# Nystrom attention with a mixing MLP: PSUM columns in runs, the pseudo-inverse in 32x32 blocks, another decode of the weights

## The chip, the cores and the metric

The kernel runs on one core of one Trainium2 chip. The metric is the device time of one execution in microseconds. Before the change three runs took 1086.55, 1086.78 and 1087.39 us, so the median is 1086.78 us. One further execution was profiled; the durations below come from it.

## The reference

The reference has two parts. The first is attention through 32 landmarks per head (8 batches, 8 heads, 576 tokens, 64 columns per head):

```python
A = sm(q, k_lm); Bm = sm(q_lm, k_lm); C = sm(q_lm, k)      # 576x32, 32x32, 32x576
Z = Bm.transpose(0, 1, 3, 2) / (norm_1(Bm) * norm_inf(Bm) + 1e-06)
for _ in range(6):
    Z = 2 * Z - Z @ Bm @ Z                                  # pseudo-inverse of Bm
attn = A @ Z @ C @ v
```

The second takes the heads side by side as `x` (8 x 576 x 512), adds the real part of its two-dimensional Fourier transform, normalises each row and puts it through a two-layer MLP (512 to 2048 to 512) with a residual:

```python
u = x + real(fft(fft(x, axis=1), axis=2))
out = u + relu(layernorm(u) @ w_ch1) @ w_ch2
```

The weights arrive as 64-bit floats.

## The kernel before

**Numbers.** Large products are made of three 16-bit matmuls each: a value is kept as a high half and a low half (`split`, line 208: ScalarE writes the high half with a scale, VectorE subtracts it and writes the low half), and `mm3` (line 203) multiplies high by high, high by low and low by high. The landmark part is 32-bit.

**Three strands.** Generators run side by side under a planner with a clock of its own (`run`, line 845): `attention` (priority 1), which calls `tokens` for a batch and spawns its `landmarks`; `weights` (priority 2); `mlp` (priority 3), which fills what is left of TensorE. Only TensorE's order is written out by the planner; the other engines' instructions stand in about the order in which the strands issue them, and each engine works its own queue in order. The planner's costs are those of `Timed` and `mm`; `till` says how long a strand waits before it comes back for a result.

**Weights** (`weights`, line 232). The 2 x 16 pieces of the two matrices (128 x 512 each) are decoded from 64-bit to 32-bit floats. For each piece ScalarE takes the magnitude of the high words into a `row` buffer, GpSimd raises it to a floor (`MIN64`), and VectorE does three integer operations: a shift by 3 and mask, an or with the top two bits, an or with the low word shifted by 29. After the next piece ScalarE sums the magnitudes of each row of the decoded piece (`bound`), which gives the power of two by which a matrix is scaled. When all of the first matrix is decoded, `scale(0)` makes that factor, and from then on one piece of the first matrix is halved (`halve`: one `split`) with each piece of the second that is decoded. After the last piece comes `scale(1)`, and then the 16 pieces of the second matrix are halved one after the other. The halves of piece f overwrite the place where the source of piece f - 1 lay, so that a high half cannot be written before the halving ahead of it is done.

**Attention, tokens** (`tokens`, line 346). Softmax rows, transposes, and the Fourier transform along the tokens: for each of two parts x and two groups g, `mm3` writes 160 columns into a PSUM tile twice, even columns and odd columns (`pss[g][:, o:320:2]`), with tables `t1`; then the 32 left-over tokens are added over all 320 columns (`t1t`), and the result is split into `CS`. That is 24 matmuls of 160 columns in a batch, 12 for each part.

**Attention, landmarks** (`landmarks`, line 477). `B` (32 x 32 per head, four heads below each other in the 128 partitions, two groups) and `C` are made; then B is laid out block-diagonally as `Bbd` (128 x 128), transposed by TensorE to `BT`, `E = I - c B B^T` is made as 128 x 128 block-diagonal matrices, and six rounds multiply E with `RE` (E's 32 columns of each head and the 64 columns of the right-hand side C v); VectorE spreads the new E over the block diagonal again each time. The last product is with `Bbd`. Everything behind it in the batch (the matrices `Wx`, `Wt`, `WC`, then `mix`, `norm`) waits for that.

**MLP** (`mlp`, line 777). 18 steps of 256 tokens, each with 8 times 24 matmuls of 256 columns (`h`) and 8 times 12 of 512 columns (`acc`). The first product needs the first matrix in halves and normalised rows of batch 0, the second needs the second matrix in halves.

## Time and profile before

| | |
|---|---|
| median of three runs | 1086.78 us |
| the profiled execution | 1085.87 us |
| its span, first to last instruction | 1084.1 us |
| TensorE busy | 995.0 us of the span |
| VectorE busy | 621.2 us |
| ScalarE busy | 350.8 us |
| GpSimd busy | 166.4 us |
| mean granted TensorE clock | 0.959 |

The profiled execution lies 0.9 us below the median, and 1.8 us of its time lie outside the span. In the profile PE is TensorE, PEld its weight loads, DVE VectorE, ACT ScalarE, POOL GpSimd. A row of a group names line, engine, operation, output and inputs by the program's tile names, shapes, count, then busy time in us and the mean in ns of one. Nearly all instructions carry the lines of helpers (196 matmul, 201 transpose, 121 the timed engines), so that groups are told apart by their tiles: `t<-`/`at<-t,mid` are the 160-column products, `at<-RE,E` a round of the inverse, `w<-w,wsc` a halving, `row<-row` of 128x512 the shift (DVE) or the floor (POOL) of the decode, `row<-w,row` and `w<-w,row` the two or-operations. A 32-bit matmul is recorded as two instructions. Times in a timeline are from the span's start, and the start of the next row says when an engine was free for it.

### The profile page before, as it was taken

The page shows a single profiled execution, that of the slowest core. Times are in us where ns is not written, and L with a number is a line of the kernel's source. Part 1 is how long each engine was busy: PE and PEld are TensorE (multiplying, and loading weights), DVE is VectorE, ACT ScalarE, POOL GpSimd, SP SyncE. Part 2 cuts the span into 40 slices and gives each one's busy share as a digit, 9 for nine tenths or more (in the row PEclk, how much of TensorE's full clock was granted, in tenths as well). Part 3 has the DMA queues.
Part 4 walks back from the last instruction along what each step waited for, and adds up shares of the span by engine and source line. Part 5 has one row for each costly group of instructions (what it writes and reads, how often), then busy time and mean ns, then how long its engine had stood idle before and what let it go on. Part 6 is the DMA issues. An engine that isn't in the chain of part 4 may idle for free.

```text
span 1084.1 us, 19661 instructions
## 1 busy us (share of the span) xinstructions
PE 995.0 (92%) x8062; PEld 695.2 (64%) x8062; DVE 621.2 (57%) x1673; ACT 350.8 (32%) x797; POOL 166.4 (15%) x157
## 2 busy tenths in 40 slices
PE   3245688999999999999999999999999999999998
PEld 2233554677776677766776677767676676766665
DVE  7988989768553466446646574566552563441111
ACT  4557656324231333123232332143312332111110
POOL 2764502021111020110202020112010020110000
PEclk9565799999999999999999999999999999999999
DMA  9734502222101130010402030113110000110000
GB/s 334 235 110 148 148 25 89 69 45 103 60 26 30 47 116 21 20 35 16 156 2 49 11 127 31 40 21 121 48 40 20 21 1 21 21 41 13 17 20 20
DMA packets 71018, 68.16 MB, mean 63 GB/s; under 512 B 41360, under 2 KB 59792, under 8 KB 70800
## 3 DMA queue, kind: packets, MB, share of 16 engines
q1 hardware_dynamic: 70928, 66.91, 20.0%
q8 instruction: 63, 1.03, 0.4%
q14 instruction: 27, 0.22, 0.1%
HBM read 48.02 MB, written 9.44 MB: 53 GB/s over the span
## 4 chain that ended last, share of the span: by engine, by line
PE 84%; DVE 11%; ACT 2%; issue 1%; DMA 1%; POOL 1%; SPq 0%; ACTq 0%; POOLq 0%
PE h L196 33%; PE acc L196 33%; PE at L196 16%; DVE w L121 3%; DVE row L121 2%; PE at L201 2%; DVE mid L121 1%; DMA w<-w_dram 1%; ACT mid L121 1%; ACT row L121 1%; DVE u L121 1%; DVE big L121 0%; ACT w L121 0%; DVE lm L121 0%; DVE asum L121 0%
## 5 line engine op out<-in xcount | busy, mean ns | idle before, releaser
L196 PE MATMUL h<-unT,w 128*128 128x256 f16 x3456 | 413.9, 274 | 17.5 <-DMA unT<-row 13.4
L196 PE MATMUL acc<-w,h 128*128 128x512 f16 x1680 | 395.1, 379 | 0.0
L196 PEld LDWEIGHTS <-w 128*128 128x128 f16 x3456 | 337.5, 99 | 88.5 <-DMA unT<-row 14.2
L196 PEld LDWEIGHTS <-h 128*128 128x128 f16 x1680 | 161.8, 98 | 160.9 <-issue 4.1
L121 DVE SCALAR_TENSOR_TENSOR h<-h 128x512 f16<-128x512 f32 x140 | 96.3, 688 | 246.7 <-ACT h L121 246.3
L121 ACT ACTIVATE h<-h 128x512 f16<-128x512 f32 x140 | 83.4, 596 | 359.0 <-PE h L196 358.6
L121 POOL TENSOR_TENSOR r<-ve,mhalf 128x2 f32<-128x2 f32 (+1 forms) x20 | 13.8, 690 | 417.5 <-DVE ve L121 417.4
L121 POOL TENSOR_SCALAR row<-row 128x512 f32<-128x512 f32 x32 | 54.9, 1729 | 57.1 <-ACT row L121 45.9
L196 PEld LDWEIGHTS <-mid 128*128 128x128 f16 x432 | 50.8, 119 | 18.4 <-issue 7.9
L121 POOL TENSOR_TENSOR mid<-mid,asum 128x512 f32<-128x512 f32 x14 | 14.8, 1055 | 276.9 <-DVE asum L121 276.9
L196 PEld LDWEIGHTS <-big 128*128 128x128 f16 (+1 forms) x768 | 40.1, 102 | 25.9 <-DVE big L121 10.8
L121 POOL TENSOR_TENSOR row<-row 128x512 f16<-128x512 f32 (+1 forms) x44 | 45.1, 1038 | 36.1 <-ACT row L121 36.1
L121 ACT CAST row<-row 128x512 f16<-128x512 f32 (+1 forms) x44 | 23.3, 558 | 71.6 <-DVE row L121 69.9
L121 DVE SCALAR_TENSOR_TENSOR row<-at,scw,row 128x262 f32<-128x262 f32 (+1 forms) x48 | 21.3, 486 | 43.7 <-ACT row L121 29.9
L121 DVE TENSOR_REDUCE lm<-big 128x32 f32<-128x576 f32 (+1 forms) x48 | 44.0, 943 | 3.9 <-DMA big<-k_dram 3.5
L121 ACT ACTIVATE row<-w 128x512 f32<-128x512 f32 x54 | 34.4, 642 | 33.1 <-DVE w L121 21.1
L196 PE MATMUL at<-RE,E 128*128 128x96 f32 (+1 forms) x192 | 30.8, 285 | 12.1 <-DVE RE L121 12.1
L196 PEld LDWEIGHTS at<-RE,E 128*128 128x128 f32 x192 | 28.4, 202 | 17.8 <-DVE RE L121 13.9
L121 DVE SCALAR_TENSOR_TENSOR u<-at,scw,row 128x128 f32<-128x128 f32 (+3 forms) x120 | 38.9, 388 | 0.0
L196 PE MATMUL at<-mid,big 128*128 128x262 f16 (+1 forms) x288 | 34.4, 288 | 4.6 <-DVE mid L121 2.3
L121 POOL TENSOR_TENSOR mid<-mid 128x256 f32<-128x256 f32 (+1 forms) x32 | 33.0, 1035 | 21.0 <-ACT mid L121 12.2
L121 DVE SCALAR_TENSOR_TENSOR u<-acc,wsc,u 128x512 f32<-128x512 f32 x36 | 26.8, 745 | 12.0 <-PE acc L196 11.7
(166 smaller groups left out, 1005.1 us busy)
## 6 DMA issues: line engine op xcount, KB each, us to landing
w<-w_dram SPq DMA_DIRECT2D x22, 512.0 KB, 5.7
big<-v_dram SPq DMA_DIRECT2D x16, 640.0 KB, 8.6
big<-q_dram SPq DMA_DIRECT2D x16, 584.0 KB, 5.2
big<-k_dram SPq DMA_DIRECT2D x16, 576.0 KB, 4.4
out_dram<-u SPq DMA_DIRECT2D x36, 256.0 KB, 2.0
big<-w_dram SPq DMA_DIRECT2D x10, 512.0 KB, 5.7
unT<-row SPq DMA_TRANSPOSE x72, 2.4
t<-t_dram SPq DMA_DIRECT2D x1, 1048.0 KB, 9.3
```

Source lines behind the costliest of these rows:

```text
L121: return call(out, *args, **kw)
L196: self.nc.tensor.matmul(out, a, b, start=start, stop=stop, skip_group_check=True)
L201: self.nc.tensor.transpose(out, a, ident)
```

## The change

There are four parts. The first stands in `tokens`: even and odd columns are written as two runs of 160, and the split puts them in turn again through access patterns; the table `t1t` has its columns in the same order.

```diff
-        t1t[:, x] = trig(fn, REST * 2, freqs, S)
+        t1t[:, x] = trig(fn, REST * 2, freqs[0::2] + freqs[1::2], S)
...
-                    mm3(pss[g][:, o:320:2], lambda y: Fs[g][:, y, 128 * i : 128 * i + 128],
+                    mm3(pss[g][:, 160 * o : 160 * o + 160], lambda y: Fs[g][:, y, 128 * i : 128 * i + 128],
...
-                split(CS[:, g, 0, x], CS[:, g, 1, x], pss[g][:, 0:320], 2.0**-15)
+                split(
+                    *(CS[:, g, y, x].rearrange("p (t o) -> p o t", o=2) for y in range(2)),
+                    pss[g][:, 0:320].rearrange("p (o t) -> p o t", o=2), 2.0**-15,
+                )
```

The second takes the pseudo-inverse out of `landmarks` into a strand `inverse` of its own, which starts as soon as B is normalised. It works on 32 x 32 blocks, each head's product being a matmul of its own on its own rows and columns of TensorE's array, and it carries E and the polynomial P, not the right-hand side; the block-diagonal matrix is made once, at the end (`Gbd`). `landmarks` waits for it and multiplies with the right-hand side `R`.

```diff
+        def blocks(out, a, b):
+            for g in range(2):
+                for i in range(4):
+                    rows = slice(32 * i, 32 * i + 32)
+                    mm(out[rows, g], a[rows, g], b[rows, g], share=0.25)
...
+        V.transpose(BT, B)
...
+        for it in range(6):
+            yield self.till(EP, banks=1, more=NM)
+            c0, c1 = (0 if it < 5 else 32), (64 if it > 0 else 32)
+            ps = two(self.psum(), 64)
+            blocks(ps[:, :, c0:c1], EP[:, :, 0:32], EP[:, :, c0:c1])
+            nEP = sm.tile([P, 2, 64], F32, name="EP", bufs=3)
+            if it < 5:
+                A.copy(nEP[:, :, 0:32], ps[:, :, 0:32])
+            if it == 0:
+                V.tensor_tensor(nEP[:, :, 32:64], EP[:, :, 0:32], diag, ALU.add)
+            else:
+                V.tensor_tensor(nEP[:, :, 32:64], EP[:, :, 32:64], ps[:, :, 32:64], ALU.add)
+            EP = nEP
...
-                mm(ps[:, 96 * g + c0 : 96 * g + 96], E[:, g].rearrange("p a b -> p (a b)"), RE[:, g, c0:])
...
-                V.tensor_tensor(E, wide(pv[:, :, 0:32], 32), m4g(32), ALU.mult)
-                A.copy(nRE[:, :, 0:32], pv[:, :, 0:32])
-            V.tensor_tensor(nRE[:, :, 32:96], RE[:, :, 32:96], pv[:, :, 32:96], ALU.add)
```

The third is the decode. ScalarE's magnitude takes a scale of 2^-112, which shifts the exponent, so that GpSimd's floor and the mask go, the sign alone is or-ed in, and the second or works in place. `bound` goes; GpSimd adds the shifted magnitudes of a matrix's 16 pieces column by column into `tops` (tile `wmax`), and `scale` takes the maximum of that.

```diff
-            A.activation(mag, self.wraw[i].rearrange("p (m x) -> p m x", x=2)[:, :, 1].bitcast(F32), AF.Abs)
-            self.G.tensor_scalar(mag, mag, MIN64, None, ALU.max)
+            A.activation(mag, self.wraw[i].rearrange("p (m x) -> p m x", x=2)[:, :, 1].bitcast(F32), AF.Abs, scale=2.0**-112)
...
-            A.activation(mags[i], slots[w][f + 1], AF.Abs, accum_out=am[w][:, f : f + 1])
...
-            V.tensor_reduce(a2, am[w], AX.X, ALU.max)
+            V.tensor_reduce(a2, tops[w], AX.X, ALU.max)
...
-            V.tensor_scalar(x, x, 3, 0x3FFFFFFF, ALU.logical_shift_left, ALU.bitwise_and)
-            V.scalar_tensor_tensor(x, top, -0x40000000, x, ALU.bitwise_and, ALU.bitwise_or)
-            V.scalar_tensor_tensor(dst.bitcast(I32), low, 29, x, ALU.logical_shift_right, ALU.bitwise_or)
-            if i > 0:
-                bound(i - 1)
+            V.tensor_scalar(x, x, 3, None, ALU.logical_shift_left)
+
+            self.G.tensor_tensor(tops[w], tops[w], mags[i], ALU.add)
+            V.scalar_tensor_tensor(dst.bitcast(I32), top, -0x80000000, x, ALU.bitwise_and, ALU.bitwise_or)
+            V.scalar_tensor_tensor(dst.bitcast(I32), low, 29, dst.bitcast(I32), ALU.logical_shift_right, ALU.bitwise_or)
```

The fourth is the halving of every second piece, 8 in each matrix: ScalarE scales the piece in place, ScalarE copies the high half, GpSimd subtracts.

```diff
-            self.split(hl[w][f][:, 0], hl[w][f][:, 1], slots[w][f + 1], sc[:, w : w + 1])
+            hi, lo, src = hl[w][f][:, 0], hl[w][f][:, 1], slots[w][f + 1]
+            if f % 2 == 0:
+                self.split(hi, lo, src, sc[:, w : w + 1])
+            else:
+                A.activation(src, src, AF.Copy, scale=sc[:, w : w + 1])
+                A.copy(hi, src)
+                self.G.tensor_tensor(lo, src, hi, ALU.subtract)
```

The change moves instructions. On TensorE, in batch 0 between the end of the token softmax (`kbd`) and the first 160-column products (`t_108`), the order before was this; `RE,E` are rounds of the inverse, `ident,mid` and `ident,row` transposes.

```order
L196 MATMUL at<-kbd,big 64x64
L196 MATMUL at<-RE,E 128x96 x2
L201 MATMUL at<-ident,mid 128x128 x8
L196 MATMUL at<-RE,E 128x96 x2
L201 MATMUL at<-ident,row 128x128
L196 MATMUL at<-RE,E 128x96 x4
L196 LDWEIGHTS mid
L196 MATMUL at<-t_108,mid 128x160
```

At the same place it is now this; `EP` are rounds of the inverse in blocks, eight matmuls each.

```order
L195 MATMUL at<-kbd,big 64x64
L200 MATMUL at<-ident,mid 128x128 x4
L195 MATMUL at<-EP 32x64 x8
L200 MATMUL at<-ident,mid 128x128 x4
L200 MATMUL at<-ident,row 128x128
L195 MATMUL at<-EP 32x64 x16
L195 LDWEIGHTS mid
L195 MATMUL at<-t_108,mid 128x160
```

Two wide matmuls became eight small ones at about the same distance from the work around them; nothing else moved here.

On VectorE, where the first matrix is decoded, two pieces at a time, before: `row<-row` is the shift, `row<-w_74,row` the first or, `w_73<-w_74,row` the second.

```order
L121 TENSOR_SCALAR row<-row 128x512 x2
L121 SCALAR_TENSOR_TENSOR row<-w_74,row 128x512 x2
L121 SCALAR_TENSOR_TENSOR w_73<-w_74,row 128x512 x2
L121 TENSOR_SCALAR row<-row 128x512 x2
L121 SCALAR_TENSOR_TENSOR row<-w_74,row 128x512 x2
L121 SCALAR_TENSOR_TENSOR w_73<-w_74,row 128x512 x2
```

Now, at the same place:

```order
L120 TENSOR_SCALAR row<-row 128x512 x2
L120 SCALAR_TENSOR_TENSOR w_73<-w_74,row 128x512 x2
L120 SCALAR_TENSOR_TENSOR w_73<-w_74,w_73 128x512 x2
L120 TENSOR_SCALAR row<-row 128x512 x2
L120 SCALAR_TENSOR_TENSOR w_73<-w_74,row 128x512 x2
L120 SCALAR_TENSOR_TENSOR w_73<-w_74,w_73 128x512 x2
```

The three operations stand as they stood; the first or now writes the piece itself, and the second reads and writes it.

On GpSimd, from the first halvings to the normalisation of batch 0 (`r`, then two `row<-row` of a pair of row tiles), before; `TENSOR_SCALAR row<-row` is the floor.

```order
L121 TENSOR_TENSOR row<-row 128x128
L121 TENSOR_SCALAR row<-row 128x512 x10
L121 TENSOR_TENSOR r_869<-ve,mhalf 128x2
L121 TENSOR_SCALAR row<-row 128x512
L121 TENSOR_TENSOR row<-row 128x512 x2
```

Now `wmax` are the sums and `w_73` the low halves of every second piece of the first matrix:

```order
L120 TENSOR_TENSOR w_73<-w_73 128x512
L120 TENSOR_TENSOR wmax_127<-wmax_127,row 128x512
L120 TENSOR_TENSOR r_887<-ve,mhalf 128x2
L120 TENSOR_TENSOR w_73<-w_73 128x512
L120 TENSOR_TENSOR wmax_127<-wmax_127,row 128x512
L120 TENSOR_TENSOR row<-row 128x512
L120 TENSOR_TENSOR wmax_127<-wmax_127,row 128x512
L120 TENSOR_TENSOR row<-row 128x512
```

The floors, which stood ahead of VectorE's shift and came in rows of up to ten, are gone; the sums stand behind the shift, and the subtractions stand among them. Further on, after `scale(1)`, eight `w_74<-w_74` stand on a queue that held nothing at that place before.

More of the change, by code (lines that the diff above doesn't have):

```diff
@@ L23 @@
 K13 = 2.0**13
-MIN64 = float(np.array([897 << 20], np.int32).view(np.float32)[0])
 TCH = 2
@@ L236, in weights @@
         slots = [[t[:, i] for i in range(NF + 1)] for t in whole]
-        am = [self.cp.tile([P, NF], F32, name=f"wmax{w}") for w in range(2)]
+        tops = [self.cp.tile([P, 512], F32, name=f"wmax{w}") for w in range(2)]
+        for t in tops:
+            nc.gpsimd.memset(t, 0.0)
         hl = [[t.bitcast(F16).rearrange("p (y m) -> p y m", y=2) for t in ss] for ss in slots]
@@ L293, in weights @@
                 yield max(0.0, max(self.V.free, self.G.free) - self.now - WT)
-        bound(2 * NF - 1)
         yield from scale(1)
@@ L475, in tokens, with inverse @@
         st["tokens"] = [*st["AT"], CS]
+    def inverse(self, st, nrm, nci):
+        mm, sm, V, A = self.mm, self.sm, self.V, self.A
+        B = nrm[:, :, 0, :]
+        diag = self.diag32.unsqueeze(1).broadcast_to([P, 2, 32])
+        BT = sm.tile([P, 2, 32], F32, name="BT", bufs=1)
+        V.transpose(BT, B)
[4 more added lines that the diff above has]
+                    mm(out[rows, g], a[rows, g], b[rows, g], share=0.25)
+        two = lambda t, m: t[:, 0 : 2 * m].rearrange("p (g m) -> p g m", g=2)
+        yield self.till(BT, nci, banks=1)
+        ps = two(self.psum(), 32)
+        blocks(ps, BT, BT)
+        EP = sm.tile([P, 2, 64], F32, name="EP", bufs=3)
+        for g in range(2):
+            V.scalar_tensor_tensor(EP[:, g, 0:32], ps[:, g], nci[:, g : g + 1], self.diag32, ALU.mult, ALU.add)
+        for it in range(6):
[11 more added lines that the diff above has]
+            EP = nEP
+        yield self.till(EP, banks=1)
+        ps = two(self.psum(), 32)
+        blocks(ps, EP[:, :, 32:64], B)
+        Gbd = sm.tile([P, 2, 4, 32], F32, name="Gbd", bufs=1)
+        V.tensor_tensor(
+            Gbd, ps.unsqueeze(2).broadcast_to([P, 2, 4, 32]), self.mask4.unsqueeze(1).unsqueeze(3).broadcast_to([P, 2, 4, 32]), ALU.mult
+        )
+        st["Gbd"] = Gbd
     def landmarks(self, b, st):
@@ L481, in landmarks @@
         loads, qbd, lm = st["loads"], st["qbd"], st["lm"]
[L482 to L483 removed]
         Bd = sm.tile([P, 2, 32], F32, name="Bd")
[L485 removed]
+        R = sm.tile([P, 2, 64], F32, name="R")
         Ces, crs = [], []
@@ L509, in landmarks @@
         )
+        yield self.till(nrm, banks=1)
+        psn = self.psum()
+        mm(psn[:, 0:128], self.ones_bd.rearrange("p a b -> p (a b)"), nrm.rearrange("p g x m -> p (g x m)"))
+        cm = self.small(4, "cm")
+        V.tensor_reduce(cm, psn[:, 0:128].rearrange("p (x m) -> p x m", m=32), AX.X, ALU.max)
+        ci = self.small(2, "ci")
+        cmv = cm.rearrange("p (g x) -> p g x", x=2)
+        V.tensor_tensor(ci, cmv[:, :, 0], cmv[:, :, 1], ALU.mult)
+        V.tensor_scalar(ci, ci, 1e-6, None, ALU.add)
+        V.reciprocal(ci, ci)
+        nci = self.small(2, "nci")
+        V.tensor_scalar(nci, ci, -1.0, None, ALU.mult)
+        self.spawn(self.inverse(st, nrm, nci))
         while b == 1 and self.seconds < NF // 2 - HB:
@@ L538, in landmarks @@
             crs.append(cr)
-        yield self.till(nrm)
-        psn = self.psum()
-        mm(psn[:, 0:128], self.ones_bd.rearrange("p a b -> p (a b)"), nrm.rearrange("p g x m -> p (g x m)"))
-        cm = self.small(4, "cm")
-        V.tensor_reduce(cm, psn[:, 0:128].rearrange("p (x m) -> p x m", m=32), AX.X, ALU.max)
-        ci = self.small(2, "ci")
-        cmv = cm.rearrange("p (g x) -> p g x", x=2)
-        V.tensor_tensor(ci, cmv[:, :, 0], cmv[:, :, 1], ALU.mult)
-        V.tensor_scalar(ci, ci, 1e-6, None, ALU.add)
-        V.reciprocal(ci, ci)
-        nci = self.small(2, "nci")
-        V.tensor_scalar(nci, ci, -1.0, None, ALU.mult)
-        Bbd = sm.tile([P, 2, 4, 32], F32, name="Bbd", bufs=1)
-        V.tensor_tensor(Bbd, wide(nrm[:, :, 0, :], 32), m4g(32), ALU.mult)
-        yield self.till(Bbd, Ces[0])
-        pst = self.psum()
-        for g in range(2):
-            tr(pst[:, 128 * g : 128 * g + 128], Bbd[:, g].rearrange("p a b -> p (a b)"), self.ident)
-        BT = sm.tile([P, 2, P], F32, name="BT", bufs=1)
-        A.copy(BT.rearrange("p g m -> p (g m)"), pst[:, 0:256])
+        yield self.till(Ces[0])
         ETs = []
@@ L571, in landmarks @@
             if g == 0:
-                yield self.till(BT, Ces[1])
-                pse = self.psum()
-                for i in range(2):
-                    mm(pse[:, 128 * i : 128 * i + 128], BT[:, i], BT[:, i])
-                E = sm.tile([P, 2, 4, 32], F32, name="E")
-                for i in range(2):
-                    V.scalar_tensor_tensor(
-                        E[:, i].rearrange("p a b -> p (a b)"), pse[:, 128 * i : 128 * i + 128], nci[:, i : i + 1],
-                        self.ident, ALU.mult, ALU.add,
-                    )
-                V.tensor_reduce(RE[:, :, 0:32], E.rearrange("p g a b -> p g b a"), AX.X, ALU.add)
+                yield self.till(Ces[1])
         for g in range(2):
```

26 lines of the change are left out of this document (7 added, 19 removed).

## The prediction

> **What bounds the kernel now.** I read the page's busy times, slices and chain first. The columns of the first row are busy us, share and count; each digit of the second is TensorE's busy share, in tenths, in a fortieth of the span.
>
> ```profile
> PE 995.0 (92%) x8062; PEld 695.2 (64%) x8062; DVE 621.2 (57%) x1673; ACT 350.8 (32%) x797; POOL 166.4 (15%) x157
> PE   3245688999999999999999999999999999999998
> PE 84%; DVE 11%; ACT 2%; issue 1%; DMA 1%; POOL 1%; SPq 0%; ACTq 0%; POOLq 0%
> ```
>
> There are two stages: over some eight slices TensorE fills up, and from there it is full to the end. The busy times by stretch put numbers to it (us: stretch and length, then busy time of PE, PEld, DVE, ACT, POOL, granted clock).
>
> ```profile
> 25.00:150.00 125.00, 65.95 (x538) 50.16 (x538) 115.62 (x247) 78.34 (x178) 64.41 (x41) 0.67 0.47 150
> 150.00:200.00 50.00, 42.63 (x369) 25.26 (x369) 40.24 (x112) 26.24 (x56) 6.92 (x8) 0.97 0.15 49
> 250.00:1000.00 750.00, 748.71 (x6196) 527.63 (x6195) 397.18 (x1110) 208.95 (x482) 82.42 (x90) 1.00 0.15 45
> ```
>
> From 25 to 150 us VectorE works 115.6 of 125 us: it decodes the weights and does batch 0. From 250 to 1000 us TensorE works 748.7 of 750. So a microsecond of TensorE's work saved in a batch after the first is a microsecond of time, whatever the other engines do there, and the first stage counts by when VectorE is through with the second matrix (`scale(1)`), since the second MLP product starts behind it. I sum the two stages apart. Batch 0's TensorE work lies under VectorE's and counts nothing; batches 1 to 7 count.
>
> **The 160-column products.** TensorE's order in time (start, us, then the group) for one part x, and two neighbours:
>
> ```profile
> 192.46 1.79 PE L196 MATMUL at<-t,mid 128*128 128x160 f16 x12
> 194.18 0.58 PE L196 MATMUL at<-t1t,row 64*128 64x320 f16 x6
> 215.56 1.52 PE L196 MATMUL at<-mid,big 128*128 128x262 f16 x12
> 216.93 1.47 PE L196 MATMUL at<-Wx,mid 128*128 128x256 f16 x12
> 218.23 0.81 PE L196 MATMUL acc<-w,h 128*128 128x512 f16 x3
> ```
>
> Twelve products of 160 columns hold TensorE for 1.72 us, 143 ns each. Twelve of 262 columns take 1.37 us, 114 ns each, 0.44 ns a column; twelve of 256 columns written in pieces of 32 take 1.30 us, 0.42 ns a column. So pieces are no cost; what the slow group alone has is a write to every other column, at twice the time per column. In runs, 160 columns should take 70 ns, and 6 for the change to the next shape that the 143 contain too: 76. That saves 67 ns x 24 x 7 batches = 11.2 us.
>
> The Trainium skill's "PSUM — Partial Sum Buffer" (its specification table) has lines of 8 bytes and says that a pattern with gaps slows matmuls significantly, which the row bears out. Its "TensorE: Matmul & The Clock Gate", section "Back-to-back issue gap", speaks against the full gain: with a weight load ahead of each matmul it gives about 81 ns at 128 columns and 131 at 512, so as an estimate some 84 at 160, and the saving would be 9.9 us. Against that stands a row of this trace, further down (`kbd,big`), where 24 matmuls of 64 columns with full weight loads take 0.71 us, 30 ns each; the sum stays with the rows.
>
> ScalarE and VectorE write `CS` with gaps of one half now; both are idle at times from 250 us on, which hides it. Uncovered, 32 splits at even twice their row would not matter before VectorE ran full.
>
> **The inverse on TensorE.** One batch in the full stage, before:
>
> ```profile
> 250.63 0.38 PE L201 MATMUL at<-ident,Bbd 128*128 128x128 f32 x2
> 250.85 0.71 PE L201 MATMUL at<-ident,mid 128*128 128x128 f32 x5
> 253.76 0.61 PE L196 MATMUL at<-BT 128*128 128x128 f32 x4
> 254.21 0.71 PE L201 MATMUL at<-ident,mid 128*128 128x128 f32 x5
> 254.85 0.90 PE L196 MATMUL at<-big,mid 128*32 128x64 f32 x40
> 255.68 1.48 PE L196 MATMUL h<-unT,w 128*128 128x256 f16 x12
> 257.93 0.87 PE L196 MATMUL at<-kbd,big 128*128 128x64 f16 x24
> 258.64 0.82 PE L196 MATMUL h<-unT,w 128*128 128x256 f16 x6
> 259.94 0.58 PE L196 MATMUL at<-RE,E 128*128 128x96 f32 x4
> 260.36 1.89 PE L196 MATMUL acc<-w,h 128*128 128x512 f16 x8
> ```
>
> Removed: the transposes 0.22 us, `BT` 0.45, six rounds of 0.42: 3.19 us a batch. Added: 64 block matmuls, 128 records. The nearest row is `big,mid`, 32-bit, 32 columns of the array: 40 records in 0.83 us, 20.8 ns each, with the change of shape in it. At that price 128 records are 2.66 us, so 0.53 us less a batch, 3.7 us in seven. The blocks are narrower in rows too, and half of the groups have only 32 columns, so half that price is the one bound (12.8 us saved); the other is one and a half times it, for eight changes of shape where there was none: 4.0 us a batch, 5.6 us lost in all. Eight short groups are each covered by the MLP's work around them as the rounds were, and `inverse` starts ahead of C, so nothing waits longer for `Gbd`.
>
> **VectorE's work in the first stage.** The groups by shape (busy us, mean ns):
>
> ```profile
> L121 DVE TENSOR_TENSOR E<-at,mask 128x256 f32<-128x256 f32 x40 | 16.7, 417 | 8.2 <-PE at L196 8.1
> L121 DVE TENSOR_TENSOR RE<-RE,at 128x128 f32<-128x128 f32 x48 | 13.5, 280 | 6.9 <-ACT RE L121 5.2 <-PE at L196 1.7
> L121 DVE TENSOR_REDUCE RE<-E 128x64 f32<-128x256 f32 x8 | 4.7, 592 | 0.0
> L121 DVE SCALAR_TENSOR_TENSOR E<-at,nci,ident 128x128 f32<-128x128 f32 x16 | 5.2, 344 | 0.8 <-PE at L196 0.8
> L121 DVE TENSOR_TENSOR nrm<-Bd,bs 128x64 f32<-128x64 f32 x8 | 1.8, 220 | 0.1
> L121 DVE TENSOR_REDUCE asum<-mid 128x16 f32<-128x512 f32 x16 | 10.9, 680 | 4.6 <-ACT mid L121 4.5
> L121 DVE SCALAR_TENSOR_TENSOR w<-w,wsc 128x512 f16<-128x512 f32 x32 | 24.9, 777 | 3.0 <-ACT w L121 2.9
> ```
>
> Batch 0's inverse gives up 5 x 417 + 6 x 280 + 592 + 2 x 344 = 5.0 us (spreading B over the diagonal and spreading the result cost the same) and takes nine small operations, which I price at the 220 of a 128x64 row: 2.0. Two reductions over 512 columns, where there were two over 16, add at most 2 x 680 = 1.4. Eight halvings of the first matrix go to ScalarE and GpSimd: 8 x 0.75 (their median, below) = 6.0. Sum -7.6; neighbours overlap by 0.08 us (below, 111.43 starts ahead of the end of 109.98 + 1.53), and 12 instructions fewer take back 1.0: -6.6 us. ScalarE loses 32 row sums there and gains 8 scalings and copies; at 78 of 125 us it stays behind VectorE.
>
> **What GpSimd does to VectorE.** The decode's two rows of means, the spreads (min/median/max) of the same tiles, and five moments of the two engines:
>
> ```profile
> L121 DVE TENSOR_SCALAR row<-row 128x512 int32<-128x512 int32 x32 | 17.2, 554 | 2.2 <-POOL row L121 2.2
> L121 DVE SCALAR_TENSOR_TENSOR w<-w,row 128x512 int32<-128x512 int32 x22 | 17.9, 820 | 0.0
> L121 DVE TENSOR_SCALAR row<-row x32: 408/420/1370, 11.1 to 142.1; 128x512 int32<-128x512 int32 x32
> L121 DVE SCALAR_TENSOR_TENSOR w<-w,row x22: 639/684/1303, 12.9 to 135.9; 128x512 int32<-128x512 int32 x22
> L121 DVE SCALAR_TENSOR_TENSOR w<-w,wsc x32: 730/746/1099, 87.7 to 189.4; 128x512 f16<-128x512 f32 x32
> 107.85 1.37 DVE L121 TENSOR_SCALAR row<-row 128x512 int32<-128x512 int32 x1 [0.37 <-POOL row L121]
> 109.98 1.53 DVE L121 SCALAR_TENSOR_TENSOR w<-big,row 128x512 int32<-128x512 int32 x1
> 111.43 0.88 DVE L121 SCALAR_TENSOR_TENSOR row<-at,scw,row 128x262 f32<-128x262 f32 x2
> 107.79 1.15 POOL L121 TENSOR_TENSOR row<-row 128x512 f16<-128x512 f32 x1
> 109.67 1.29 POOL L121 TENSOR_TENSOR row<-row 128x512 f16<-128x512 f32 x1 [0.73 <-ACT row L121]
> ```
>
> The shift loses 0.13 us on average against its median, the second or 0.14, a halving 0.03: with 32, 22 and 32 of them that is 4.3 + 3.0 + 1.0 = 8.3 us. That is about 0.23 us for each of GpSimd's 36 wide operations beside the decode (32 floors, 4 subtractions for rows). The two moments at 107.8 and 109.7 are dearer: beside a GpSimd operation with two inputs, the shift took 0.95 us and the or 0.85 us over their medians, to the end of GpSimd's. The change takes 32 floors away, and puts in 32 sums and 8 subtractions, all with two inputs, and each sum becomes ready just as VectorE starts the two ors: 44 such operations. At 0.23 the loss is 10.1 us (1.8 more than now), at 0.85 it is 37.4 (29.1 more), at nothing 8.3 less. I take 0.45, nearer to the lower row, since most floors held nothing up (the or's median is untouched by 32 of them) and two fifths of VectorE's work here is neither decode nor halving (32 x (0.42 + 0.68 + 0.68) + 16 x 0.75 = 69 of 115.6 us are): 19.8, so +11.5 us. With the work saved, `scale(1)` comes 4.9 us later.
>
> **Halving the second matrix.** VectorE's rows are a halving each, with ScalarE's between them:
>
> ```profile
> 151.22 0.75 DVE L121 SCALAR_TENSOR_TENSOR w<-w,wsc 128x512 f16<-128x512 f32 x1 [0.79 <-ACT w L121]
> 152.76 0.75 DVE L121 SCALAR_TENSOR_TENSOR w<-w,wsc 128x512 f16<-128x512 f32 x1 [0.79 <-ACT w L121]
> ```
>
> A piece takes 1.54 us, strictly in turn, and TensorE, which needs two for 12 products, waits here. A pair takes 3.08 now. In the new pair ScalarE's 0.79 and VectorE's 0.75 stay; the in-place scaling lies beside VectorE's part; then come a copy, which I take at 0.7 of ScalarE's 0.79, and a subtraction of 1.15 on GpSimd: 3.4. Behind the waiting next high half on ScalarE stand batch 1's exponentials and copies, with TensorE behind them. Four pairs come before batch 1's products fill the gaps: 4 x 0.32 = +1.3 us.
>
> **The sum.** -11.2 - 3.7 + 4.9 + 1.3 = -8.7 us against the profiled 1085.87 us: 1077.2. The median of the runs is 0.9 us higher than the profiled one, so I name 1078.1; the rivals' times have the 0.9 in them too. What a measurement of this kernel can tell from no change is about 0.2%, 2.2 us.
>
> **The rivals.** First, slower: the sums hold VectorE up in full. The place is the decode from 25 to 150 us, the price 0.85 us an operation: `scale(1)` comes 29.1 - 6.6 = 22.5 us later, and 1085.87 - 14.9 + 22.5 + 1.3 + 0.9 = 1095.7 us. It decides from 0.65 us an operation on, where 44 of them (28.5 us) eat 8.3 + 6.6 + 14.9 - 1.3. For it speak the two moments, against it the 0.23 of all together. The Trainium skill's "SBUF — State Buffer", section "Who interferes with whom", states this as the rule: a VectorE instruction with two inputs in SBUF and a GpSimd one that reads SBUF exclude each other, and the later one blocks fully. The two moments agree; the untouched median of the or beside 32 floors does not.
>
> Second, GpSimd waits instead and VectorE is not held up, 0.2 us an operation or less: a loss of 8.8 us, `scale(1)` 6.1 us earlier, 1067.1; at nothing 1058.3, unless the first MLP product then bounds. For it speaks that GpSimd was held up itself: its subtraction took 1.15 us at 107.8 and 1.29 at 109.7.
>
> Third, the change does not do what it says on TensorE: gaps in the write were not the cause, and the 11.2 us stay: 1089.3.
>
> Fourth, the blocks of different heads run one after another. Four columns of blocks side by side are in the 20.8 ns; alone they would be 83 a record at 64 columns, 16 records 1.33 us, and half at 32: 8.0 us a batch, 4.8 more, 33.6 in all beside the 3.7 lost: 1115.4 us. Against it stands that row; products that use only some of the rows run side by side too (`t1t,row`, 320 columns in 0.58 us for six).
>
> **How the numbers follow.** My forecast has 0.62, GpSimd waiting 0.18, VectorE held up 0.14, the write not the cause 0.04, blocks in turn 0.02. Within the forecast 0.45 us an operation is known to some 0.1 (4.4 us) and the inverse to some 6, so that it ends above 1084.6, the 2.2 us below no change, in one case of ten: 0.56 faster, 0.03 the same, 0.03 slower. With the others: faster 0.56 + 0.18 + 0.03 = 0.77, the same 0.03 + 0.03 + 0.02 = 0.08, slower 0.03 + 0.08 + 0.02 + 0.02 = 0.15. The range reaches down into the second case, to 1062, and up to the middle of the first, to 1092.
>
> **What would show it.** In the profile after: twelve products of 160 columns in 0.9 us; the rounds `EP` at 0.2 to 0.5 us for 16 records; TensorE's products in a batch 1.6 plus 0.5 us shorter; the shift and the ors with means over 0.6 and 0.9 us if VectorE is held up, at their medians if not; the last reduction of `wmax` some 5 us later; pairs of halvings 3.4 us apart. The forecast is wrong if that reduction moves by over 15 us either way, if the products keep 1.72 us, or if TensorE shows new idle times after 250 us, which the sum holds for nothing.

## The result and the profile after

The changed kernel takes 1110.72 us (median of 4 runs, 1108.61 to 1112.49) where the kernel before takes 1086.86 beside it: a ratio of 1.0219 (95% interval 1.0206 to 1.0233), 23.9 us slower. The forecast was 1078.1, so even the sign is wrong. The profiled execution of the changed kernel took 1108.61 us, with a span of 1106.8.

First the page of the changed kernel: busy us, share and count of each engine, and TensorE's busy tenths in fortieths of the span.

```profile
PE 984.0 (89%) x8846; PEld 670.3 (61%) x8846; DVE 624.1 (56%) x1617; ACT 338.4 (31%) x741; POOL 183.4 (17%) x175
PE   2234377899999999999999999999999999999998
```

TensorE works 11.0 us less than before (984.0 against 995.0) and the span is 22.7 us longer, so the time went into waits. The busy times by stretch say where (us: stretch and length, then busy time of PE, PEld, DVE, ACT, POOL, granted clock, the DMA engines' share and GB/s):

```profile
25.00:150.00 125.00, 49.79 (x514) 35.43 (x515) 115.21 (x226) 61.92 (x129) 63.12 (x45) 0.62 0.45 144
250.00:1000.00 750.00, 741.54 (x6802) 509.15 (x6800) 397.44 (x1125) 213.65 (x488) 87.42 (x94) 1.00 0.16 46
```

There are two places. Up to 150 us VectorE is as busy as before (115.2 of 125 us) though it has 21 instructions fewer, and TensorE got only 49.8 us of work done in that time, 16 less. And from 250 us on, where TensorE had 1.3 idle us in 750, it has 8.5. The last reduction of `wmax`, which stood at 146.5 us, comes at 163.3, and the second MLP product starts at 173.55 us where it started at 151.24:

```profile
L120 DVE TENSOR_REDUCE wm<-wmax x2: 672/672/673, 82.8 to 163.3; 128x1 f32<-128x512 f32 x2
132.96 0.39 PE L195 MATMUL h<-unT,w 128*128 128x256 f16 x1 [16.99 <-DMA unT<-row]
173.55 0.38 PE L195 MATMUL acc<-w,mid 128*128 128x512 f16 x1 [1.58 <-ACT w L120]
```

**The start.** Two pieces of the first matrix on VectorE in time (start, us, then the group), and GpSimd's sums beside them; `w<-w,row` is the first or, `w<-w,w` the second, `row<-row` the shift:

```profile
36.56 3.43 DVE L120 SCALAR_TENSOR_TENSOR w<-w,row 128x512 int32<-128x512 int32 x2
39.92 1.28 DVE L120 SCALAR_TENSOR_TENSOR w<-w,w 128x512 int32<-128x512 int32 x2
41.12 0.75 DVE L120 TENSOR_SCALAR row<-row 128x512 int32<-128x512 int32 x2
41.79 3.41 DVE L120 SCALAR_TENSOR_TENSOR w<-w,row 128x512 int32<-128x512 int32 x2
...
36.45 2.99 POOL L120 TENSOR_TENSOR wmax<-wmax,row 128x512 f32<-128x512 f32 x2 [0.43 <-DVE row L120]
41.68 2.98 POOL L120 TENSOR_TENSOR wmax<-wmax,row 128x512 f32<-128x512 f32 x2 [2.24 <-DVE row L120]
```

A sum starts 0.11 us ahead of the first or that stands beside it, lasts 1.5 us, and the or takes 1.7 us, where it takes 0.69 with no sum beside it (next section). VectorE is held inside the or, not ahead of it: the groups below had next to no idle time in front (the last figure, 0.0 and 0.1 us). The second or and the shift, which fall between two sums, take 0.64 and 0.38. A pair of pieces takes 41.79 - 36.56 = 5.23 us. Over the whole decode the groups of the first or, by shape, say the same (busy us, mean ns):

```profile
L120 DVE SCALAR_TENSOR_TENSOR w<-w,row 128x512 int32<-128x512 int32 x22 | 25.9, 1189 | 0.0
L120 DVE SCALAR_TENSOR_TENSOR w<-big,row 128x512 int32<-128x512 int32 x10 | 13.4, 1345 | 0.1
L120 DVE TENSOR_SCALAR row<-row 128x512 int32<-128x512 int32 x32 | 15.6, 504 | 0.6 <-ACT row L120 0.6
```

The last row is the shift, the first operation of a piece: in 32 pieces VectorE waited 0.6 us for a row of magnitudes.

**The full stage.** TensorE in batch 2, and what it waited for longest after 200 us (us in total, times, longest):

```profile
263.05 0.38 PE L195 MATMUL at<-nrm,ones_bd 128*128 128x128 f32 x2
263.37 2.16 PE L195 MATMUL at<-big,qbd 128*64 128x288 f32 x16
266.84 0.27 PE L200 MATMUL at<-ident,amax 128*4 128x128 f32 x1 [1.31 <-ACT mid L120]
...
PE at L200 <- ACT mid L120: 10.1, 7, 1.9
```

The products of C (`big,qbd`) end at 265.53, and the transpose of `amax`, which needs nothing of theirs, waits 1.31 us for ScalarE's exponential `mid`, which reads them. What links the two is room: the tiles `at` have four PSUM buffers, C takes four, and the transpose wants a fifth. In the kernel before, the column sums of `nrm` and this transpose stood together, 1.9 us of MLP products behind C's end:

```profile
243.64 2.14 PE L196 MATMUL at<-big,qbd 128*64 128x288 f32 x16
...
247.68 0.40 PE L196 MATMUL at<-nrm,ones_bd 128*128 128x128 f32 x2
247.92 0.27 PE L201 MATMUL at<-ident,amax 128*4 128x128 f32 x1
```

The change moved the column sums ahead of C, and the transpose, which is not in the diff at all, slid up to C's end. Start to start, it stands 1.72 us or more behind C's last product in every batch from 2 to 7: six waits, 8.2 us of idle time together. The seventh in the last row, of 1.9 us, is in batch 1, ahead of other transposes (`ident,mid`).

### The profile page after: what moved, and what is told of

Same layout as the page of the kernel before. It is cut to its first block, busy times and chain, and to the rows that moved or that the text cites. A ratio compares the mean times of both kernels' runs of the same rounds, so it can differ in the third digit from the quotient of the medians.

```text
span 1106.8 us, 21166 instructions
## 1 busy us (share of the span) xinstructions
PE 984.0 (89%) x8846; PEld 670.3 (61%) x8846; DVE 624.1 (56%) x1617; ACT 338.4 (31%) x741; POOL 183.4 (17%) x175
## 4 chain that ended last, share of the span: by engine, by line
PE 81%; DVE 11%; ACT 3%; issue 2%; POOL 1%; DMA 1%; SPq 0%; ACTq 0%; POOLq 0%; DVEq 0%
PE h L195 33%; PE acc L195 33%; PE at L195 13%; DVE w L120 5%; PE at L200 2%; ACT w L120 1%; DMA big<-k_dram 1%; DVE row L120 1%; POOL w L120 1%; DVE cmx L120 1%; DVE mid L120 1%; ACT mid L120 1%; DVE big L120 0%; DVE u L120 0%; DVE lm L120 0%
## 5 line engine op out<-in xcount | busy, mean ns | idle before, releaser
L120 POOL TENSOR_TENSOR wmax<-wmax,row 128x512 f32<-128x512 f32 x32 | 51.0, 1593 | 65.2 <-DVE row L120 53.4
L120 POOL TENSOR_TENSOR mid<-mid,asum 128x512 f32<-128x512 f32 x14 | 15.5, 1106 | 246.2 <-DVE asum L120 241.1
L195 PEld LDWEIGHTS <-mid 128*128 128x128 f16 x432 | 38.1, 101 | 28.2 <-issue 18.6
L195 PE MATMUL at<-kbd,big 128*128 128x64 f16 (+1 forms) x480 | 18.6, 201 | 19.5 <-DVE big L120 19.4
L120 POOL TENSOR_TENSOR mid<-mid 128x256 f32<-128x256 f32 (+1 forms) x32 | 31.3, 981 | 19.0 <-ACT mid L120 10.5
L200 PE MATMUL at<-ident,mid 128*128 128x128 f32 (+1 forms) x144 | 23.4, 291 | 9.8 <-DVE mid L120 5.4
L195 PE MATMUL at<-EP 32*32 32x64 f32 (+1 forms) x768 | 20.0, 221 | 10.1 <-DVE EP L120 7.9
```

The lines of the kernel that those rows point to most:

```text
L120: return call(out, *args, **kw)
L195: self.nc.tensor.matmul(out, a, b, start=start, stop=stop, skip_group_check=True)
L200: self.nc.tensor.transpose(out, a, ident)
```

## The experiments

The theory: three things cost the time, each at its own price: the sums on GpSimd hold VectorE up, the halves of the odd pieces on GpSimd ("odd halves" from here on) are late, and the transpose waits for a PSUM buffer; the products in runs gain what was forecast. The rivals are that the delay of the start comes from the rows that the sums hold, and that the waits of the full stage are moved rather than made.

**Sums on ScalarE.** The running sums become row sums of the same magnitudes:

```
-            self.G.tensor_tensor(tops[w], tops[w], mags[i], ALU.add)
...
+            A.activation(mags[i], mags[i], AF.Abs, accum_out=tops[w][:, f : f + 1])
```

> Starts from the changed kernel; only the 32 running sums of the magnitudes go from GpSimd to ScalarE, as row sums of the same magnitudes (so the bound is a row sum of one piece, no longer a sum over the pieces; its power of two alone matters). Theory: the sums hold VectorE up by 0.7 to 0.85 us each, which made the first h product come 20 us later; without them about 20 us go, 1088 to 1092 us against 1110.7, the first or that reads a magnitude falls from a mean of 1.5 us to 0.7, and the first h product starts at 112 to 116 us again. Rival A (the rows are the cause: a sum holds its row buffer, and with it the next load and magnitude, and ScalarE holds it just as long): within 5 us of 1110.7. Rival B (the delay comes from halving the odd pieces on ScalarE and GpSimd): within 5 us of 1110.7, too, but the or falls to 0.7.

Measured: 1082.26 us, ratio to the kernel before 0.995 (0.9933 to 0.9968). So 28.5 us go, more than the theory said: 0.89 us of time for each of 32 sums. The second ors of two pieces of the first matrix on VectorE in that run, and the group of the first or:

```profile
33.57 0.69 DVE L120 SCALAR_TENSOR_TENSOR w<-w,w 128x512 int32<-128x512 int32 x1
...
35.10 0.69 DVE L120 SCALAR_TENSOR_TENSOR w<-w,w 128x512 int32<-128x512 int32 x1
...
L120 DVE SCALAR_TENSOR_TENSOR w<-w,row 128x512 int32<-128x512 int32 x22 | 15.1, 686 | 0.0
```

From piece to piece it is 1.53 us here, and 5.23 / 2 = 2.61 with the sums: 1.08 us a sum where nothing else breaks the rhythm. The rows are not the cause: ScalarE reads each row once more here, as GpSimd did, and in the changed kernel VectorE waited only 0.6 us for rows. The odd halves are still on GpSimd in this run, so it is not they that went.

**One input in place of two.** GpSimd still passes over every magnitude, but without the sum:

```
-            self.G.tensor_tensor(tops[w], tops[w], mags[i], ALU.add)
+            self.G.tensor_scalar(tops[w], mags[i], 0.0, None, ALU.max)
```

> Starts from the changed kernel; each of the 32 sums is replaced by a copy of the magnitude into the same tile, floored at 0: a GpSimd operation with one input, at the same place, that holds the same row and lasts as long or longer (one-input operations of this size took 1.73 us in the kernel before, sums 1.59). It leaves out the sum, so the scale comes from the last piece's magnitudes alone. Theory (VectorE's two-input instruction and GpSimd's two-input one shut each other out): the first or falls to means of 0.7 to 0.9 us, and 12 to 20 us go: 1091 to 1099 us. Rivals (any GpSimd operation of that length holds VectorE up, or the row buffers do): the or stays at 1.4 us or over, or the time stays within 5 us of 1110.7.

Measured: 1095.37 us, ratio 1.0069 (1.0042 to 1.0097). VectorE and GpSimd at the same place, then the groups of the first or and of GpSimd's operation:

```profile
37.01 1.69 DVE L120 SCALAR_TENSOR_TENSOR w<-w,w 128x512 int32<-128x512 int32 x2
...
40.91 1.69 DVE L120 SCALAR_TENSOR_TENSOR w<-w,w 128x512 int32<-128x512 int32 x2
...
34.94 9.21 POOL L120 TENSOR_SCALAR wmax<-row 128x512 f32<-128x512 f32 x5
...
L120 DVE SCALAR_TENSOR_TENSOR w<-w,row 128x512 int32<-128x512 int32 x22 | 17.0, 783 | 0.0
L120 POOL TENSOR_SCALAR wmax<-row 128x512 f32<-128x512 f32 x32 | 57.7, 1802 | 51.5 <-DVE row L120 40.6 <-DVE wx_e L120 5.4 <-DVE asum L120 4.5
```

GpSimd works without a break here, 1.80 us an operation, longer than a sum, and two pieces take VectorE 40.91 - 37.01 = 3.90 us, 1.95 each: 0.42 more than with no work on GpSimd beside it, where a sum costs 1.08. In time it is (1095.37 - 1082.26) / 32 = 0.41 us against 0.89. So neither GpSimd's being busy nor the length of its operation sets the price; the form does, as far as these two forms tell. One thing differs beside the form: a sum starts just ahead of an or each time, the one-input operations follow each other at their own pace, and no run holds that fixed. The form is what the prediction mixed up: its lower row, 0.23, came from floors with one input, its upper one, 0.85, from operations with two. (Nor did the floors hold up as little as 0.23: in the kernel before, at this place, the shifts of two pairs of pieces start at 31.63 and 35.80 us, so a piece took 2.09 us beside floors, 0.55 more than 1.53.)

**Plain halves.** All pieces are halved on ScalarE and VectorE again; the sums stay on GpSimd.

```
-            if f % 2 == 0:
+            if True:
                 self.split(hi, lo, src, sc[:, w : w + 1])
```

> Starts from the changed kernel; all pieces are halved on ScalarE and VectorE again, none on GpSimd. Theory: in the first stage it is even (eight halvings of 0.75 us come back to VectorE, and eight subtractions of GpSimd that held it up by about as much go), and the second matrix gets 3 to 4 us faster (its first to last product with the rows of batch 0 took 19.8 us in the changed kernel and 16.3 before): 1105 to 1109 us against 1110.7. Rival (VectorE is the bound of the first stage, so eight halvings more cost their 6.0 us): 1113 to 1117.

Measured: 1100.66 us, ratio 1.0129 (1.0108 to 1.015): the odd halves cost 10.0 us beside the sums, and neither theory nor rival has that. TensorE's first products of the MLP, and the last reduction:

```profile
126.27 0.39 PE L195 MATMUL h<-unT,w 128*128 128x256 f16 x1 [11.59 <-DMA unT<-row]
167.56 0.59 PE L195 MATMUL acc<-w,mid 128*128 128x512 f16 x1 [1.77 <-ACT w L120]
L120 DVE TENSOR_REDUCE wm<-wmax x2: 672/674/675, 82.6 to 161.5; 128x1 f32<-128x512 f32 x2
```

The first product of the MLP is 6.7 us earlier, and the second matrix's first product 6.0, although VectorE has eight halvings more to do before it. The halvings that went to GpSimd were thus no relief in the changed kernel.

**Odd halves without the sums.** Two mends together (sums on ScalarE, and the wait for a PSUM tile that comes next), with the odd halves on GpSimd kept:

> The kernel with the three mends, but with every odd piece halved on ScalarE and GpSimd as in the changed kernel. With the sums on GpSimd the odd halves cost 10.0 us (1110.7 against 1100.7). Theory: part of that is GpSimd's queue, in which sums and subtractions stand in line with the rows' subtractions ahead of the first MLP product; without the sums that part goes, and what is left is some 4 us, 1071 to 1075 (the run with sums on ScalarE alone, 1082.3, less the 9.5 of the waits is 1072.8). Rival (each subtraction holds VectorE up by as much as a sum, whatever else is in the queue): 1077 to 1080.

Measured: 1073.84 us, ratio 0.9876 (0.9858 to 0.9894), against 1068.58 for the same kernel with plain halves (below): 5.3 us. So the odd halves cost about half as much without the sums. The last reduction of `wmax` and TensorE's products with the second matrix for batch 0 (first and last start) in this run, then with plain halves:

```profile
L120 DVE TENSOR_REDUCE wm<-wmax x2: 151/153/155, 66.8 to 135.1; 128x1 f32<-128x16 f32 x2
L195 PE MATMUL acc<-w,mid x48: 376/380/632, 144.6 to 167.3; 128*128 128x512 f16 x48
...
L120 DVE TENSOR_REDUCE wm<-wmax x2: 156/156/156, 65.9 to 137.7; 128x1 f32<-128x16 f32 x2
L195 PE MATMUL acc<-w,mid x48: 376/379/634, 143.7 to 160.8; 128*128 128x512 f16 x48
```

Without the sums the relief is there: the reduction comes 2.6 us earlier with the odd halves. It is gone by the first product with the second matrix, which comes 0.9 us later, and then the 48 products, which wait for the halves of the second matrix, take 22.7 us against 17.1: 5.6 us more. That covers the price of 5.3. What makes it 10.0 beside the sums is not separated.

**A wait for a PSUM tile.** One line makes the scheduler put the transpose of `amax` where a buffer is free:

```
         yield self.till(am, more=AM)
+        yield self.till(banks=1)
```

> Starts from the changed kernel; one line makes the scheduler put off the transpose of amax until one of the four PSUM tiles is free, so that MLP products stand between C's products and it. Theory: the waits of 1.72 us ahead of that transpose in batches 2 to 7 (10.6 us in six) come from C's four tiles holding all four buffers, since the column sums of nrm moved ahead of C; they go, and nothing else is late: 1099 to 1102 us against 1110.7. Rival (the transpose is needed that early, and the batch behind it comes later by as much): waits of the same sum elsewhere after 200 us, 1108 to 1112.

Measured: 1101.17 us, ratio 1.0129 (1.0105 to 1.0152), so 9.5 us go. TensorE in batch 2, and its longest wait after 200 us:

```profile
267.08 2.16 PE L195 MATMUL at<-big,qbd 128*64 128x288 f32 x16
269.17 0.82 PE L195 MATMUL acc<-w,h 128*128 128x512 f16 x3
269.83 1.47 PE L195 MATMUL h<-unT,w 128*128 128x256 f16 x12
271.14 0.27 PE L200 MATMUL at<-ident,amax 128*4 128x128 f32 x1
...
PE at L200 <- ACT mid L120: 1.9, 1, 1.9
```

Fifteen MLP products stand in the place of the wait. The six waits ahead of the transpose of `amax` are gone, and the one of 1.9 us that is left is that of batch 1, ahead of other transposes. The waits were made by the order, and they did not move elsewhere: from 250 to 1000 us TensorE is busy 749.75 us in this run, against 741.54.

**The products in runs alone**, on the kernel before:

```
-                    mm3(pss[g][:, o:320:2], ...
+                    mm3(pss[g][:, 160 * o : 160 * o + 160], ...
```

> Starts from the kernel before; only the 160-column products are written in runs (with the splits that undo it on ScalarE and VectorE). Theory: twelve products fall from 1.72 to 0.93 us, 0.79 us for each of 14 groups in seven batches, 11.1 us, and nothing takes it back: 1075 to 1077 us against 1086.5. Rival (the splits, which write every other column now and took ScalarE 526 ns where they took 435, or the next stage, give some of it back): 1078 to 1083.

Measured: 1074.28 us, ratio 0.988 (0.9857 to 0.9903): 12.3 us faster, all that was forecast and nothing given back.

```profile
277.45 0.99 PE L196 MATMUL at<-t,mid 128*128 128x160 f16 x12
```

Twelve products took 1.79 in this view before, and 0.99 now.

**The inverse alone**, on the kernel before (the functions `inverse` and `landmarks` of the changed kernel):

> Starts from the kernel before; only the inverse is changed to blocks of 32 (with the column sums of nrm ahead of C). Theory: TensorE's own work falls by 0.72 us in each of seven batches (3.19 to 2.47), 5.0 us, VectorE saves some 3 us in the first stage, and six waits of 1.72 us ahead of the transpose of amax come in (10.3 us) where the waits there cost 3.7 less 0.8 before: 1086 to 1090 us against 1086.9, so this part alone gains nothing. Rival (the waits come from the later start or from the other parts): no such waits, 1078 to 1080.

Measured: 1095.52 us, ratio 1.0072 (1.0052 to 1.0093). The six waits came in as the theory said, but the part costs 9.0 us, where 0 to 4 were expected. Then the same with the wait for a PSUM tile:

> Starts from the kernel before; the inverse in blocks of 32, and the transpose of amax put off until one of the four PSUM tiles is free. With the inverse alone the time was 1095.5 us against 1086.5. Theory: that run's six waits of 1.72 us ahead of the transpose go, as they did in the changed kernel (9.5 us): 1085 to 1087. Rival (the inverse in blocks is dear by itself, by its sixteen short matmuls in a group): over 1091.

Measured: 1086.62 us, ratio 0.9996 (0.9985 to 1.0007). The waits were 8.9 us; without them the new inverse is worth nothing, although a group of sixteen records (0.36 or 0.26 us from start to start) is shorter than the round of 0.42 that it replaced. TensorE in that run shows why:

```profile
255.63 1.46 PE L196 MATMUL acc<-w,h 128*128 128x512 f16 x6
257.02 0.43 PE L196 MATMUL at<-EP 32*32 32x64 f32 x16
257.38 1.47 PE L196 MATMUL acc<-w,h 128*128 128x512 f16 x6
258.68 0.82 PE L196 MATMUL h<-unT,w 128*128 128x256 f16 x6
259.34 1.26 PE L196 MATMUL at<-kbd,big 128*128 128x64 f16 x36
...
282.83 0.82 PE L196 MATMUL h<-unT,w 128*128 128x256 f16 x6
283.58 0.33 PE L196 MATMUL at<-nrm,EP 32*32 32x32 f32 x16
283.84 1.38 PE L196 MATMUL h<-unT,w 128*128 128x256 f16 x11
```

From start to start, six `acc` products take 1.39 us ahead of a group of blocks and 1.30 ahead of an `h` product; six `h` products take 0.75 ahead of blocks and 0.66 ahead of others. Going over to blocks costs TensorE 0.09 us, which lie between the start of the last full product and that of the first block; the row of the six products is no longer for it (1.46 and 1.47 us). With it a group of 64 columns is 0.36 + 0.09 = 0.45 us and one of 32 columns 0.26 + 0.09 = 0.35, and a batch 4 x 0.45 + 4 x 0.35 = 3.2 us, just what the old inverse took. The old rounds need no such addition: in the kernel before, three `acc` products take 0.65 us ahead of `RE,E` (259.29 to 259.94), the usual time, although those too go from 16-bit to 32-bit. The row that the prediction took as nearest did have one, ahead of its own start: `big,mid`, with 32 columns of the array, came 1.42 us after the start of the twelve `h` products at 255.68, where twelve usually take 1.31.

```profile
257.10 0.90 PE L196 MATMUL at<-big,mid 128*32 128x64 f32 x40
```

What happens in the 0.09 us, the change itself or a weight load that the change uncovers, is not separated.

**Three mends at once**: sums on ScalarE, plain halves, the wait for a PSUM tile.

> The changed kernel with three mends at once: sums on ScalarE, all pieces halved on ScalarE and VectorE, the transpose of amax put off until a PSUM tile is free. Theory: the three causes add up: 1082.3 (sums on ScalarE) less 9.5 (the waits) less 2 to 5 (the halves): 1067 to 1072 us, faster than both kernels. Rival (they overlap: with a start that is earlier the full stage has the same waits elsewhere): 1074 to 1082.

Measured: 1068.58 us, ratio 0.9831 (0.9812 to 0.9849). That is in the theory's range, but the prices do not add up: apart, the three mends took away 28.5 + 10.0 + 9.5 = 48.0 us, together 1110.72 - 1068.58 = 42.1. The theory had the odd halves at 2 to 5 us, and beside the two other mends they cost 5.3, so its range held, by luck in part, although they cost 10.0 in the changed kernel. The sums and the odd halves share some 5 us of their prices.

**The old inverse in the mended kernel.** Since the new inverse was worth nothing by itself, the last run takes the old one back:

> The kernel with the three mends (1068.6 us), but with the inverse of the kernel before (and without the wait for a PSUM tile, which the old order doesn't need). Theory: a group of sixteen block products costs TensorE 0.35 us (32 columns) or 0.45 us (64) from the product before it to the product behind it, since going over to it takes 93 ns more (309 ns after an acc product where 216 is usual); a batch's eight groups are 4 x 0.35 + 4 x 0.45 = 3.2 us, and the old inverse is 3.2 us as well. So the inverse in blocks is worth nothing on TensorE, and the time stays within 2 us: 1067 to 1071. Rival (the blocks save 0.72 us in each of seven batches, and 3 us of VectorE's first stage): 1073 to 1077.

Measured: 1063.56 us, ratio 0.9786 (0.9767 to 0.9805), the best of all and 5.0 us better than with the new inverse; neither theory said so. The full stage is about the same: from the first product of batch 3 (`lm,qbd`) to the last of all it takes 706.0 us with the old inverse and 705.0 with the new one. The difference lies ahead of it. TensorE's first product with the second matrix starts at 139.50 us, where it started at 143.72 with the new inverse, and another 1.9 us come in up to batch 3. The row of that product with the old inverse, and VectorE's waits of one kind for TensorE from 15 to 140 us (total, times, longest) with the new inverse, with the old one, and with the new one in the run on the kernel before:

```profile
139.50 0.38 PE L195 MATMUL acc<-w,mid 128*128 128x512 f16 x1 [1.77 <-ACT w L120]
...
DVE cmx L120 <- PE at L195: 1.4, 3, 0.7
...
DVE cmx L120 <- PE at L195: 0.4, 2, 0.3
...
DVE cmx L121 <- PE at L196: 1.5, 3, 0.7
```

VectorE saves instructions with the new inverse, but stops more often for a product, with the decode queued behind it: 4.3 us in its four largest waits for TensorE's products against 1.0 in the two of the old inverse. These stops do not settle it: all of VectorE's waits in the stretch come to 12.2 and 8.9 us, a difference of 3.3, and in the run on the kernel before, with the PSUM wait, the same stops (3.2 us for `cmx`, `cm` and `ab_e`) cost nothing: the first product with the second matrix starts at 151.39 us there, and at 151.24 in the kernel before. Why the new inverse costs 5.0 us in the mended decode stays open.

## Why the prediction was wrong

The parts can be priced by a chain of runs, each of which differs from the next in one part. From the kernel before (1086.6): products in runs, 1074.28; the new decode with its sums on ScalarE and plain halves, 1063.56; the new inverse with the wait for a PSUM tile, 1068.58; the odd halves, 1073.84; the sums on GpSimd, 1101.17; without the wait for a PSUM tile, 1110.72.

| part | forecast, us | measured along the chain, us |
|---|---|---|
| products in runs | -11.2 | -12.3 |
| decode: no floors, sums on GpSimd, their reductions | +12.9 | -10.7 + 27.3 = +16.6 |
| odd halves, first and second matrix | -4.7 | +5.3 |
| inverse, on TensorE, on VectorE, and its order | -6.7 | +5.0 + 9.5 = +14.5 |
| overlap of fewer instructions | +1.0 | |
| sum | -8.7 | +24.1 |

The measured column adds up by construction, and its split depends on the order of the chain: next to the sums the odd halves cost 10.0, and without the odd halves the sums would cost some 22.6 us (1100.66 - 9.5 - 1068.58, an estimate, as no run has that kernel). In either order the two largest misses are the inverse with its waits, 21 us off (16 by the run of the inverse alone, +9.0), and the odd halves, 10 or 15 us off. The decode as a whole was forecast within 1 to 4 us, but that is partly luck: the sums that came were dearer than forecast, and so were the floors that went, if the 10.7 us are theirs, which no run shows by itself; the two errors offset each other.

The **products in runs** were right, in mechanism and size: -11.2 was forecast, twelve products "0.9 us" came out at 0.93 from start to start, and the run of this part alone gave -12.3 (-10.5 to -15.5 by its interval). The Trainium skill's "TensorE: Matmul & The Clock Gate", section "Back-to-back issue gap", gives about 81 ns a matmul at 128 columns. The trace shows 78 ns at 160 columns, less than that for more columns, so the trace decides, as the prediction let it.

**GpSimd's hold on VectorE** had the right mechanism and the wrong size. The prediction had both ends, 0.23 us an operation and 0.85, and took 0.45, "nearer to the lower row, since most floors held nothing up". The floors have one input in SBUF and the sums two, and the rows of two-input operations were the two moments at 107.8 and 109.7, which it had quoted. Measured: 0.71 to 0.89 us of time a sum (22.6 to 28.5 us over 32), 1.08 where pieces follow each other, 0.41 for an operation with one input. The 0.23 itself was low: its sum of 8.3 us left two groups of ors out (22 first ones, `row<-w,row`, 737 ns on average against a median of 681, and ten second ones, `w<-big,row`, 767 against 682: 2.1 us more). So the first rival's mechanism held, "the sums hold VectorE up in full", beyond its point of decision at 0.65; it stopped at 1095.7 us because it had the rest as in the forecast. The Trainium skill's "SBUF — State Buffer", section "Who interferes with whom", states that a VectorE instruction with two SBUF inputs contends with a GpSimd one that reads SBUF and that the later one blocks fully. The sums come near to that: an or of 0.69 us that starts 0.11 us after a sum of 1.5 takes 1.7, where waiting for the sum's end would make 2.1. The one-input operation doesn't: it reads SBUF too, lasts 1.80 us, and holds a piece up by 0.42. And of the prediction's two moments only the or is a case for that rule; the shift at 107.85 has one input.

**VectorE's saved work** of 6.6 us was real on paper: the instructions are gone. 6.0 us of it were the eight halvings, and moving all sixteen cost 10.0 us in the changed kernel, and 5.3 without the sums, where the decode did end 2.6 us earlier. The inverse's part did not show: in the run with the inverse and the PSUM wait alone, the second matrix's first product came no earlier.

**The odd halves** are one of the two steps that failed most. A pair in the second matrix was forecast at 3.4 us (its terms make 3.24), +1.3 us in all. The first two subtractions on GpSimd in the changed kernel, and the fifth:

```profile
175.34 1.16 POOL L120 TENSOR_TENSOR w<-w 128x512 f16<-128x512 f32 x1 [14.52 <-ACT w L120]
179.06 1.16 POOL L120 TENSOR_TENSOR w<-w 128x512 f16<-128x512 f32 x1 [2.56 <-ACT w L120]
...
193.56 1.16 POOL L120 TENSOR_TENSOR w<-w 128x512 f16<-128x512 f32 x1 [2.27 <-ACT w L120]
```

The first pair takes 3.7 us, near to the forecast, but the four pairs take 4.6 on average, not 3.4; among them stand some 4 us of ScalarE's work on batch 1 (`Bd`, `klm`, `big`, `EP`). The products that wait for them take 19.8 us from first to last start, against 16.3 in the kernel before: +3.5 us, not +1.3, and 5.6 in the runs without the sums. What the sum missed altogether is the first matrix, where it had only VectorE's 6.0 us of relief: with the odd halves the first MLP product comes 6.7 us later. GpSimd's subtractions for the rows account for about half of that (they start 3.0 and 3.2 us later, at 125.44 and 128.40 us against 122.45 and 125.24, the first of them behind a sum that waits for VectorE); the rest is not shown.

**The inverse on TensorE** was forecast at -3.7 us and is worth nothing there. The nearest row, 20.8 ns a record, "with the change of shape in it", was wrong on that clause: the group itself came out shorter than forecast on average (0.36 and 0.26 us, where 16 records at 20.8 ns make 0.33), but the 0.09 us for going over to blocks stand ahead of it, as they stood ahead of `big,mid` too, and eight groups pay them eight times. The upper bound, half as much again for eight changes of shape, was the right thought, and its 5.6 us the wrong size; the lower bound, half the price, is 13.0 us by its own terms and not 12.8. The Trainium skill's "TensorEngine Tiling (Array Packing)", section "Key Properties", says that a change of tiling mode drains TensorE. The 0.09 us agree with it. In the mended kernel the new inverse costs 5.0 us more, for a reason that stays open.

**The waits after 250 us** are the other step that failed most, and the one for which the sum had nothing: it said that `inverse` starts ahead of C, "so nothing waits longer for `Gbd`". That was true of `Gbd`. It did not follow the four PSUM buffers past the step that moved, and so missed the transpose of `amax`, 9.5 us. The prediction named new idle times of TensorE after 250 us as what would prove it wrong, and they are there, with the last reduction of `wmax` 16.8 us late, where 4.9 were forecast.

## What to carry to other kernels

Before a wide operation goes to GpSimd, count its inputs in SBUF and look at what VectorE does at that moment: here two inputs on both sides cost VectorE 1.08 us for a sum of 1.5, and the price must come from rows of the same form, not from a mean over all of GpSimd's work. When work leaves a busy engine, follow what waits for its result: the odd halves relieved VectorE and made TensorE wait. When a step is moved in a program, follow the buffers it takes as well as its results: the stall falls on the next one to ask for a buffer, which may stand in no line of the diff. Price a short group on TensorE from the start of the instruction before it, not from its own first start. And price parts by runs that differ in one of them, beside the others: prices taken apart need not add up, 48.0 against 42.1 us here.

## What the runs showed of the hardware

Beside the decode of the first matrix, where pieces follow each other, an operation of GpSimd with one input (1.80 us) held VectorE up by 0.42 us, and one with two inputs (1.5 us) by 1.08. Twelve products of 160 columns took 0.93 us written in runs and 1.72 written to every other column. Going from full products to blocks of 32 rows and 32 columns cost TensorE 0.09 us, whether 512-column or 256-column products stood ahead; the time lies between two starts and lengthens no row.
